# Block 0's first product partly in seven half-size products, and batch 0's local v loaded in 96 rows

## The chip, the cores and the metric

One core of one Trainium2 chip runs the kernel. The metric is the device time of one execution in microseconds (us); the kernel before has a median of 286.13 us over three runs (285.47, 286.13 and 286.18). A core has five engines that run their own instruction streams and wait for each other by semaphores: TensorE (PE, matmuls and transposes; its weight loads are listed as PEld), VectorE (DVE), ScalarE (ACT), GpSimd (POOL) and SyncE (SP). Loads and stores are issued by SP, ACT or POOL and carried out by 16 DMA engines.

## The reference

Attention with two kinds of mask, followed by a two-layer network with the activation h * tanh(softplus(h)) (Mish):

```python
# q, k, v: (8 batches, 8 heads, 576 positions, 64); w_in: 512 x 2048; w_out: 2048 x 512
scores = (q @ k.T) / sqrt(64)
mask_local   = (rel >= 0) & (rel < 32)                     # heads 0..3, rel = row - column
mask_strided = (rel >= 0) & (pos_k % 32 == pos_q % 32)     # heads 4..7
attn = softmax(where(mask, scores, -1e9))
x = concat_heads(attn @ v)            # 4608 tokens x 512
h = x @ w_in
out = (h * tanh(softplus(h))) @ w_out # 4608 x 512, float32
```

## The kernel before

The 4608 tokens are handled as 9 blocks of 512; the attention runs batch by batch (576 tokens), one batch ahead of the blocks, and writes its result transposed into `xT`, a ring of four batches. Everything is in one hand-written order (`manual_schedule`): each engine runs its instructions in the order of the program, and the attention steps of the next batch are put between the matmuls of the second product (`at`, a list of steps by position).

**Local heads.** Heads 0 to 3 work in six windows of 96 queries. A window's keys and values are 128 rows: 32 rows of the window before and its own 96. `vl` holds v in this form, one buffer for even and one for odd batches, with a column of ones after the 64 of each head (it gives the denominators). For batch 0 the windows are fetched whole, overlapping, 128 rows each: heads 0 and 1 in float32 by SP into `vl32` (L876 to L879), which GpSimd casts into `vl` (L906); heads 2 and 3 by GpSimd straight into `vl` (L899 to L903), converted on the way. The 32 rows that would lie before position 0 are set to zero (L888, L907). For the other batches `load_own_v_loc` (L172) fetches only the 96 own rows of each window into rows 32 to 127, and `share_v_loc` (L178) copies rows 96 to 127 of each window to rows 0 to 31 of the next: on GpSimd for batch 1, on ACT from batch 2 on.

**Start.** SP's queue holds two strided heads of k (`st0`) and the local v. GpSimd's queue holds, in this order: the rest of the strided k, strided q, strided v, local k and q, v of heads 2 and 3, `w_in` columns 0:512 and 512:1024, the cast, a memset, `w_in` 1024:1536 and 1536:2048, two memsets, and later the four pieces of `w_out` and the loads of batch 1. PE does some matmuls whose result nobody reads (`unread`, the tile `un`) between batch 0's transposes and scores.

**First product.** In blocks 1 to 8 the first product of most columns is done in the Strassen-Winograd way: with w_in cut in quarters a11, a12, a21, a22 (`w_quarter`: 256 rows of x's features by 768 columns) and xT cut in quarters b11 to b22 (`x_quarter`: 256 features by 256 tokens), seven products of sums (`Sw`, `Sx`, made on DVE by `sums_w_in` and `sums_x`) take the place of eight. In `mlp1` the function `product` (L557) issues one of them as matmuls of 256 columns; results are added up in the accumulators `z[1]`, `z[2]`, `z[3]` and in `z[5]` in SBUF, by ACT copies and DVE adds, and go through Mish on ACT into `gT`. In block 0 all sixteen chunks of 128 hidden columns are done directly instead: `group(g)` (L520) takes chunks 2g and 2g + 1, four matmuls of 512 columns each, and one Mish of 128 x 1024. The strided features (cc 2 and 3) come first for g = 0, 1, 2, as these are ready before the local ones. `sums_w_in()[0:3]` for block 1 is made in this time, over all 768 columns; its last sum, which overwrites a21, comes in block 1.

**Accumulators.** PSUM holds three accumulators of two banks (`acc(0)` to `acc(2)`) and two single banks (`tile_t`). In block 0 `accs = (1, 0, 2)`; group g takes `accs[g % 3]`. Batch 1's attention uses acc 0 and the single banks; the second product of block 0 (`mlp2`) uses acc 2 and acc 1.

**Around the change.** After block 0's first product ACT loads the table for the exponential. The transposes of batch 1's strided k and q (`t_step`, in `T`) follow: T[0] and T[1] at once, T[2] and T[3] after the first four matmuls of `mlp2`, all through the single banks. Then come the scores (`qk`), exponential, mask on DVE, and the products with v (`pv`).

Of the kernel before, what the change touches and what calls it, by code (L numbers as in the profile page):

```python
# [10 lines left out]
F32 = mybir.dt.float32  # L11
BF16 = mybir.dt.bfloat16
# [4 lines left out]
NW = 6  # L17
# [26 lines left out]
def kernel(ctx, tc, q, k, v, moe_w_in, moe_w_out, out):  # L44
# [18 lines left out]
    stm = consts[0:PN, 128 + WQ:128 + WQ + PN]  # L63
    loc_bias = consts[:, 128 + WQ + PN:128 + 2 * WQ + PN]
    stm_bias = consts[0:PN, 128 + 2 * WQ + PN:128 + 2 * WQ + 2 * PN]
    vl32 = const.tile([128, 4, NW, D], F32, name="vl32")
    vsr = const.tile([128, 4, CS * D], BF16, name="vsr")
    ql32 = const.tile([128, 4, CL, D], F32, name="ql32")
    kl32 = const.tile([128, 4, CL, D], F32, name="kl32")
# [36 lines left out]
    def acc(i, name):  # L106

        pool = ps_z[0] if i == 2 else ps_a
        return pool.tile([128, 2, 512], F32, tag=f"acc{i}", name=name)
# [45 lines left out]
    def spread_v_str(b, eng):  # L155
        cast(eng, vs[b % 2][0:PN, :, :, 0:D], vs_raw().rearrange("p h (j d) -> p h j d", d=D))

    def load_v_loc(b):

        w0 = 0
        if b == 0:
            w0 = 1
            nc.sync.dma_start(vl32[32:128, 0, 0, :], v[0, 0, 0:96, :])
        first = v[b, 0:1, 0:1, :].offset + (w0 * WQ - 32) * D
        src = bass.AP(v.tensor, first, [[D, 128], [WQ * D, 4 * NW - w0], [1, D]])
        nc.sync.dma_start(vl32[:].rearrange("p h w d -> p (h w) d")[:, w0:, :], src)  # L170

    def load_own_v_loc(b):  # L172
        for h in range(4):
            nc.gpsimd.dma_start(  # L174
                vl[b % 2][32:128, :, h, 0:D], v[b, h].rearrange("(w p) d -> p w d", p=WQ)
            )
# [17 lines left out]
    def cast(eng, out_, in_):  # L194
        if eng is nc.scalar:
            nc.scalar.copy(out_, in_)  # L196
        else:
            eng.tensor_copy(out_, in_)
# [32 lines left out]
                    by_tile(src[0])[:, hp].rearrange("p i e d -> p (i e d)"),  # L231
                )

    def cast_v_loc(b, eng, i0=0, i1=NW):
        for i in range(i0, i1, 3):
            cast(
                eng, vl[b % 2][:, i:i + 3, :, 0:D],
                vl32[:, :, i:i + 3, :].rearrange("p h w d -> p w h d"),
            )
        if i0 == 0:  # L240
            eng.memset(vl[b % 2][0:32, 0, :, 0:D], 0.0)


    def t_loc(b, which, hp, tr):
        src = by_head((ql if which == "q" else kl)[b % 2])
        for j in range(CL):
# [8 lines left out]
            tr[:, 0:S].rearrange("c (j p) -> c p j", j=CL),  # L255
        )

    def t_step(b, kind, which, hp, eng=None):

        eng = eng or nc.vector  # L260
        tr = tile_t("tr")[:].bitcast(BF16)
        if kind == "s":
            src = (qs if which == "q" else ks)[b % 2]
            for u in range(8):
                h, jj = 2 * hp + u // 4, u % 4
                nc.tensor.transpose(  # L266
                    tr[:, PN * u:PN * u + PN],
                    src[0:PN, h, 128 * jj:128 * jj + 128],
                    ident[0:PN, 0:PN],
                )  # L270
            dst = (qTs if which == "q" else kTs)[:, 8 * SU * hp:8 * SU * hp + 8 * SU]
            cast(
                eng, dst.rearrange("c (u n) -> c u n", u=8)[:, :, 0:PN],
                tr[:, 0:S].rearrange("c (u n) -> c u n", u=8),
            )
        else:
            t_loc(b, which, hp, tr)(eng)

    def unread(n, i_acc=None):

# [168 lines left out]
    def attn_steps(b, x, y):  # L449

        a = Attn(b)
        Q = lambda i_acc, *parts: (lambda: a.qk(parts, i_acc))
        M = lambda kd, i: (lambda: a.mask(kd, i, nc.vector))
        V = lambda kd, i: (lambda: a.pv(kd, i))
        X = lambda kd, hf: (lambda: a.xt(kd, hf))
        s0, s1, sl2, l0, l1 = ("s", 0), ("s", 1), (("s", 2), ("l", 2)), ("l", 0), ("l", 1)
        if x == y:
            T = [(lambda n=n: t_step(b, *T_ORDER[n])) for n in range(4)]

            def t_pair(which):  # L460
                tr = acc(x, "tr")
                copies = [t_loc(b, which, hp, tr[:, hp, :].bitcast(BF16)) for hp in range(2)]
                for copy, eng in zip(copies, (nc.vector, nc.scalar)):
                    copy(eng)

            return [
                T[2:4],
                [Q(x, s0), Q("t", s1), lambda: spread_v_str(b, nc.vector), M(*s0), M(*s1)],
                [],
                [V("s", 0)],  # L470
                [V("s", 1), Q(x, ("s", 2))],
                [V("s", 2), M("s", 2), lambda: t_pair("k")],
                [V("s", 3)],
                [V("s", 4), lambda: t_pair("q")],
                [V("s", 5)],
                [V("s", 6), Q(x, l0)],
                [V("s", 7), M(*l0), Q(x, l1)],
                [X("s", 0), V("l", 0), M(*l1), Q(x, ("l", 2))],
                [X("s", 1), V("l", 1), M("l", 2)],
                [V("l", 2), V("l", 3)],  # L480
                [V("l", 4), V("l", 5)],
                [lambda: a.xt_now(5, nc.vector), lambda: a.xt_later(5)],
            ], T[0:2]
        V2 = lambda kd, i, z: (lambda: a.pv2(kd, i, z))
        G = lambda kd, i: (lambda: a.mask(kd, i, nc.gpsimd))
        l2 = ("l", 2)
        now = -(-(512 * (b + 1) - S * b) // WQ)
        at = [
            [],
            [Q(x, s0), Q(y, s1), Q("t", *sl2), M(*s0), M(*s1), M("s", 2)],  # L490
            [],
            [V2("s", 0, y), G(*l2)],
            [],
            [V2("s", 2, y), Q(x, l0), Q("t", l1), G(*l0), G(*l1)],
            [],
            [V2("s", 4, y), lambda: nc.scalar.preload_act_table(AF.Mish)],
            [],
            [V2("s", 6, y)],
            [V2("l", 0, x)],
            [X("s", 0), V2("l", 2, y), X("s", 1)],  # L500
            [V2("l", 4, x), lambda: a.xt_now(now)],
            [lambda: a.xt_later(now)],
        ]
        return at
# [10 lines left out]
    def mlp1(t, accs):  # L515
# [4 lines left out]
        def group(g, ccs=(2, 3, 0, 1), ps=None, between=None):  # L520
            if g not in held:
                if ps is None:
                    tiles[g] = acc(accs[g % 3 if t == 0 else 0], "psh")
                    ps = [tiles[g][:, u, :] for u in range(2)]
                held[g] = ps
            for u in range(2):
# [13 lines left out]
            if ccs[-1] == 1 and g in tiles:  # L540
                to = gT[:, g::8, :] if t > 0 else gT[:, 2 * g:2 * g + 2, :]
                nc.scalar.activation(to, tiles[g][:], AF.Mish)  # L542
        if t == 0:
            def first_group(g):
                group(g)
                if g == 7:
                    nc.scalar.preload_act_table(AF.Exp)
            halves = [[lambda g=g, c=c: group(g, c) for g in range(3)] for c in ((2, 3), (0, 1))]
            return gT, halves[0], halves[1] + [lambda g=g: first_group(g) for g in range(3, 8)]

        z = {}
        a11, a12, s3, a22 = [w_quarter(i, j) for i in range(2) for j in range(2)]
        s1, s2, s4 = [Sw[:, i] for i in range(3)]
# [27 lines left out]
        def begin():  # L581
# [7 lines left out]
            product(both(z[3]), 0, s1, t1, first=True)  # L589
            sums_x(t, "3")  # L590
            if t == 1:
                sums_w_in()[3]()
            if 1 < t < B - 1:
                spread_v_str(t + 1, nc.vector)
            nc.scalar.copy(z[5][:], z[3][:])
# [1 line left out]
            product([y[1]], 512, a11, b11, first=True)  # L597

        y = {}

        def second():
            for n in range(2):
# [99 lines left out]
    def sums_w_in():  # L702

        a11, a12, a21, a22 = [w_quarter(i, j) for i in range(2) for j in range(2)]
        s1, s2, s4 = [Sw[:, i] for i in range(3)]
        return [
            lambda: sums(s1, a21, a22, ALU.add), lambda: sums(s2, s1, a11, ALU.subtract),
            lambda: sums(s4, a12, s2, ALU.subtract), lambda: sums(a21, a11, a21, ALU.subtract),
        ]

    def x_quarter(t, i, j):
# [157 lines left out]
    with tc.manual_schedule():  # L869
# [3 lines left out]
        st0 = g_pool.tile([128, 16, 512], BF16, tag="gT", name="st0")  # L873
        st0 = st0[0:PN].rearrange("p a b -> p (a b)").bitcast(F32)[:, 0:1024].rearrange("p (h x) -> p h x", h=2)
        nc.sync.dma_start(st0, k[0, 4:6].rearrange("h (p j) d -> p h (j d)", j=CS))
        nc.sync.dma_start(vl32[32:128, 0, 0, :], v[0, 0, 0:96, :])  # L876
        first = v[0, 0:1, 0:1, :].offset + 64 * D
        heads = vl32[:].rearrange("p h w d -> p (h w) d")
        nc.sync.dma_start(heads[:, 1:12, :], bass.AP(v.tensor, first, [[D, 128], [WQ * D, 11], [1, D]]))  # L879
        load_str(0, ks, k, 2)  # L880
        load_str(0, qs, q)
        load_early_v_str(0)
# [2 lines left out]
        Dv.memset(kTs[:, 0:16 * SU].rearrange("c (u n) -> c u n", u=16)[:, :, PN:SU], 0.0)  # L885
        Dv.memset(kTs[:, 16 * SU:], 0.0)
        Dv.memset(kTl[:, :, 0:32], 0.0)
        Dv.memset(vl32[0:32, 0, 0, :], 0.0)  # L888
        for p, n in zip(P_s, (6, 6, 4)):
            Dv.memset(p[:, :, n * PN:], 0.0)  # L890
        for p, n in zip(P_l, (5, 5, 2)):
# [1 line left out]
        for i in range(2):  # L893
            Dv.memset(vs[i][:, :, :, D:D + 1], 1.0)
            Dv.memset(vl[i][:, :, :, D:D + 1], 1.0)
        Dv.memset(vl[0][0:32, 0, :, D:D + 1], 0.0)
        Dv.memset(vl[1][0:32, 0, :, :], 0.0)

        for h in (2, 3):  # L899
            first = v[0, h:h + 1, 0:1, :].offset - 32 * D  # L900
            nc.gpsimd.dma_start(
                vl[0][:, :, h, 0:D], bass.AP(v.tensor, first, [[D, 128], [WQ * D, NW], [1, D]])
            )  # L903
        load_w_in(0, 512)
        load_w_in(512, 1024)
        cast(Po, vl[0][:, :, 0:2, 0:D], vl32[:, 0:2].rearrange("p h w d -> p w h d"))  # L906
        Po.memset(vl[0][0:32, 0, :, 0:D], 0.0)  # L907
        load_w_in(1024, 1536)
        load_w_in(1536, 2048)
        for x in (ks, qs):  # L910
            Po.memset(x[1][64:SU].rearrange("p h x -> p (h x)").bitcast(F32), 0.0)

# [41 lines left out]
        a.xt("s", 1)  # L954
        a.pv2("l", 2, 0)
        a.pv2("l", 4, 2)
        g1s[0]()
        a.xt("l", 0)
        a.xt("l", 1)
        Sc.preload_act_table(AF.Mish)  # L960
        g1s[1]()
        g1s[2]()
        for f in sums_w_in()[0:3]:
            f()
        for x in (ks, qs):
            Po.memset(x[0][64:SU].rearrange("p h x -> p (h x)").bitcast(F32), 0.0)
        load_qk_str(2)
# [92 lines left out]
```

## Time and profile before

The profiled execution took 285.53 us; its span, from the first to the last instruction, is 283.8 us.

| Engine | busy, us | share of the span |
|---|---|---|
| PE | 277.6 | 98% |
| PEld (weight loads) | 217.9 | 77% |
| ACT | 196.4 | 69% |
| DVE | 195.6 | 69% |
| POOL | 109.4 | 39% |

By stage, from the busy time of stretches of the span:

| Stretch, us | what runs | PE | DVE | ACT | POOL | moved, GB/s |
|---|---|---|---|---|---|---|
| 5.00 to 19.80 | batch 0's attention | 13.69 | 6.98 | 8.82 | 8.30 | 193 |
| 19.80 to 34.69 | block 0, first product | 14.75 | 4.33 | 9.85 | 8.43 | 201 |
| 34.69 to 56.25 | block 0, second product, with batch 1's attention | 21.46 | 17.75 | 10.97 | 11.93 | 161 |
| 56.25 to 85.32 | block 1, with batch 2's attention | 29.07 | 25.07 | 24.32 | 12.76 | 169 |

The granted TensorE clock is 1.00 throughout. A line of a timeline reads: start, duration (us), engine, source line, operation, output <- inputs, shape, count, and in brackets the idle time before it with what ended it. Matmuls overlap, so their durations add up to more than the time between their starts; the cost of one in a row of them is the distance of the starts. A line of the chain reads: start, duration, engine, tile, source line, count.

### The profile page before, as it was taken

What the parts mean: (1) busy time and instruction counts of PE and PEld (TensorE: products, weight loads), DVE (VectorE), ACT (ScalarE), POOL (GpSimd) and SP (SyncE); (2) the same over time, 40 slices, a digit from 0 to 9 for tenths busy, and PEclk for the clock granted to TensorE, in tenths of its full rate; (3) what the DMA queues carried; (4) which work ended last, traced back from release to release, by engine and by line L of the source; (5) the groups of instructions that cost most, each with busy time, mean ns of one, the idle gap of its engine ahead of it and who ended that gap; (6) DMA issues with size and microseconds to landing.
All of it is one profiled execution on the core that took longest, in us unless ns stands there. A gap on an engine that the chain in (4) does not pass through costs nothing.

```text
span 283.8 us, 7529 instructions
## 1 busy us (share of the span) xinstructions
PE 277.6 (98%) x3119; PEld 217.9 (77%) x3119; DVE 195.6 (69%) x402; ACT 196.4 (69%) x293; POOL 109.4 (39%) x129
## 2 busy tenths in 40 slices
PE   8899999999999999999999999999999999999994
PEld 3564455686898689868988898789978997888684
DVE  2283078889787777878777778777877767644742
ACT  2578653699857985798679876987798769417820
POOL 8375457308261727253726272535423500000000
PEclk9999999999999999999999999999999999999999
DMA  8999999999998999699989999999969041003004
GB/s 153 187 202 205 197 181 166 132 142 238 170 131 113 217 174 149 136 211 175 152 141 208 153 171 135 222 127 169 148 174 111 3 160 25 0 21 131 0 2 148
DMA packets 103437, 40.28 MB, mean 142 GB/s; under 512 B 85868, under 2 KB 98908, under 8 KB 103404
## 3 DMA queue, kind: packets, MB, share of 16 engines
q1 hardware_dynamic: 65004, 24.40, 50.0%
q0 software_dynamic: 38112, 15.17, 49.3%
q8 instruction: 24, 0.39, 0.7%
q10 hardware_dynamic: 288, 0.25, 0.3%
q14 instruction: 9, 0.07, 0.1%
HBM read 37.01 MB, written 9.44 MB: 164 GB/s over the span
## 4 chain that ended last, share of the span: by engine, by line
PE 92%; DMA 3%; DVE 2%; ACT 1%; issue 0%; POOL 0%; POOLq 0%
PE pso L757 31%; PE psu L562 10%; PE psh L531 10%; PE psv L562 9%; PE psb L562 8%; PE psb L531 5%; PE pso L817 4%; PE po L371 4%; PE pso L790 4%; PE ps L335 4%; DMA qs<-in_q_dram 3%; PE trx L420 1%; DVE x_s L397 1%; PE tr L248 1%; PE trx L435 1%; PE tr L266 1%
## 5 line engine op out<-in xcount | busy, mean ns | idle before, releaser
L757 PEld LDWEIGHTS <-gT 128*128 128x128 bf16 x448 | 41.9, 98 | 5.8
L562 PEld LDWEIGHTS <-w_in 128*128 128x128 bf16 x384 | 37.4, 98 | 8.4
L355 POOL TENSOR_TENSOR Pl<-Pl,consts_sb 128x960 bf16<-128x960 bf16 (+1 forms) x18 | 29.2, 1637 | 35.5 <-issue 22.5
L757 PE MATMUL pso<-w_out,gT 128*128 128x256 bf16 x336 | 41.0, 272 | 0.0
L757 PEld LDWEIGHTS <-Sg 128*128 128x128 bf16 x336 | 31.5, 98 | 4.4
L531 PEld LDWEIGHTS <-w_in 128*128 128x128 bf16 x208 | 20.2, 98 | 16.6 <-issue 0.6
L562 PEld LDWEIGHTS <-Sw 128*128 128x128 bf16 x288 | 28.1, 98 | 3.5 <-DVE Sx L665 0.3
L531 PE MATMUL psh<-xT,w_in 128*128 128x512 bf16 (+1 forms) x136 | 29.4, 366 | 0.2
L196 ACT COPY xT<-trx 128x576 bf16<-128x576 bf16 (+3 forms) x24 | 14.2, 629 | 18.4 <-PE trx L420 12.8
L757 PE MATMUL pso<-Tw,Sg 128*128 128x256 bf16 x224 | 26.7, 273 | 0.0
L196 ACT COPY osb<-pso 128x512 f32<-128x512 f32 (+1 forms) x17 | 9.4, 555 | 20.2 <-PE pso L757 10.8
L174 POOL DMA_DIRECT2D vl<-in_v_dram x28 | 20.6, 742 | 6.2 <-DMA w_out<-in_moe_w_out_dram 2.3
L571 ACT ACTIVATE gT<-psu 128x1024 bf16<-128x1024 f32 x16 | 16.4, 1025 | 8.5 <-PE psu L562 8.5
L397 DVE TENSOR_TENSOR x_s<-po,rden 72x512 bf16<-72x512 f32 x28 | 19.2, 687 | 1.0
L637 POOL COPY mark<-qTl 1x4 bf16<-1x4 bf16 x6 | 2.1, 353 | 45.9 <-DMA qTl<-ql 45.9
L542 ACT ACTIVATE gT<-psh 128x1024 bf16<-128x1024 f32 x16 | 16.2, 1024 | 4.0 <-PE psh L531 3.9
L665 DVE TENSOR_TENSOR Sg<-gT 128x256 bf16<-128x256 bf16 (+2 forms) x32 | 12.8, 422 | 8.0 <-ACT gT L571 6.7
L665 DVE TENSOR_TENSOR psu<-psb,p 128x512 f32<-128x512 f32 x16 | 11.2, 700 | 9.8 <-PE psb L562 9.0
L562 PE MATMUL psu<-xT,w_in 128*128 128x256 bf16 x128 | 17.9, 272 | 0.0
L734 DVE TENSOR_TENSOR p<-pso,p 128x512 f32<-128x512 f32 x14 | 9.6, 686 | 11.8 <-PE pso L757 11.8
L562 PE MATMUL psb<-Sx,w_in 128*128 128x256 bf16 x128 | 17.2, 272 | 0.0
L349 ACT ACTIVATE Ps<-ps 72x864 bf16<-72x864 f32 (+1 forms) x17 | 13.8, 855 | 4.2 <-PE ps L335 4.2
(141 smaller groups left out, 613.7 us busy)
## 6 DMA issues: line engine op xcount, KB each, us to landing
out_dram<-osb SPq DMA_DIRECT2D x9, 512.0 KB, 3.9
out_dram<-p SPq DMA_DIRECT2D x7, 512.0 KB, 3.0
kl<-in_k_dram SPq DMA_DIRECT2D x5, 576.0 KB, 10.2
ql<-in_q_dram SPq DMA_DIRECT2D x5, 576.0 KB, 16.0
qs<-in_q_dram POOLq DMA_DIRECT2D x8, 288.0 KB, 11.1
vsr<-in_v_dram POOLq DMA_DIRECT2D x8, 288.0 KB, 8.6
w_in<-in_moe_w_in_dram POOLq DMA_DIRECT2D x4, 512.0 KB, 9.7
w_out<-in_moe_w_out_dram POOLq DMA_DIRECT2D x4, 512.0 KB, 13.0
```

The lines of the kernel that those rows point to most:

```text
L174: nc.gpsimd.dma_start(vl[b % 2][32:128, :, h, 0:D], v[b, h].rearrange("(w p) d -> p w d", p=WQ))
L196: nc.scalar.copy(out_, in_)
L335: nc.tensor.matmul(by_e[e][:, o:o + w], lhsT=lhsT, rhs=rhs, start=not biased, stop=True, skip_group_check=biased,)
L349: nc.scalar.activation(pt[0:n, :, 0:nw], ps[0:n, :, o0:o0 + nw], AF.Exp, scale=scale)
L355: meng.tensor_tensor(out=pm, in0=pm, in1=mk[0:n, :].unsqueeze(1).unsqueeze(1).to_broadcast([n, 2, nu, w]), op=ALU.mult,)
L397: nc.vector.tensor_tensor(out=dst.rearrange("p e (h d) -> p e h d", h=4), in0=po[0:m, :, :, 0:D], in1=rden[0:m].unsqueeze(3).to_broadcast( ...
L531: nc.tensor.matmul(ps_u[:, o:o + n], lhsT=w_in[:, cc, fc * 128:(fc + 1) * 128], rhs=xT[:, cc, a:a + n], start=(cc == 2 and (o == 0 or len( ...
L542: nc.scalar.activation(to, tiles[g][:], AF.Mish)
L562: nc.tensor.matmul(p[:, 256 * j:256 * j + 256], lhsT=lhs[:, cc, f:f + 128], rhs=rhs[:, cc], start=(first and j == 0 and cc == 0), stop=(la ...
L571: nc.scalar.activation(gT[:, c:c + src.shape[1], 256 * half_t:256 * half_t + 256], src, AF.Mish,)
L665: nc.vector.tensor_tensor(out=out_, in0=in0, in1=in1, op=op)
L757: nc.tensor.matmul(ps[:, pair, :], lhsT=lhs(c, 128 * pair), rhs=rhs(c), start=(first and pair == 0 and c == 0), stop=(last and c == 7), sk ...
```

## The change

Two parts. First, batch 0's local v is fetched like the other batches' (96 rows for each window): SP brings heads 0 and 1 into a smaller `vl32`, whose rows 0 to 31 DVE sets to zero, GpSimd's two loads of heads 2 and 3 become `load_own_v_loc(0, (2, 3))`, and GpSimd copies the shared rows with `share_v_loc(0, Po)` after the cast and the `w_in` loads. The order of the four `w_in` loads becomes 512:1024, 1536:2048, 1024:1536, 0:512, and the last two no longer stand behind the memset L907, which is gone.

Second, block 0's chunks 0 to 3 and 8 to 11 are done by seven products of 512 hidden columns; groups 2, 3, 6 and 7 (chunks 4 to 7 and 12 to 15) stay direct, and come first but for group 7, which is put between the first two products and the others. The sums of w_in are cut in columns 0:512 (made before and in `first_products`, all four) and 512:768 (three in `other_products`, the last in block 1's `begin`). The sums of x for block 0 are new. Batch 1's first two transposes go through acc 0 as a pair (`t_first`) instead of the two single banks.

```diff
-        Dv.memset(vl32[0:32, 0, 0, :], 0.0)
+        Dv.memset(vl32[0:32], 0.0)
...
-        nc.sync.dma_start(vl32[32:128, 0, 0, :], v[0, 0, 0:96, :])
-        first = v[0, 0:1, 0:1, :].offset + 64 * D
-        heads = vl32[:].rearrange("p h w d -> p (h w) d")
-        nc.sync.dma_start(heads[:, 1:12, :], bass.AP(v.tensor, first, [[D, 128], [WQ * D, 11], [1, D]]))
+        nc.sync.dma_start(
+            vl32[32:128].rearrange("p h w d -> p (h w) d"),
+            v[0, 0:2].rearrange("h (w p) d -> p (h w) d", p=WQ),
+        )
...
-        for h in (2, 3):
-            first = v[0, h:h + 1, 0:1, :].offset - 32 * D
-            nc.gpsimd.dma_start(
-                vl[0][:, :, h, 0:D], bass.AP(v.tensor, first, [[D, 128], [WQ * D, NW], [1, D]])
-            )
-        load_w_in(0, 512)
-        load_w_in(512, 1024)
-        cast(Po, vl[0][:, :, 0:2, 0:D], vl32[:, 0:2].rearrange("p h w d -> p w h d"))
-        Po.memset(vl[0][0:32, 0, :, 0:D], 0.0)
-        load_w_in(1024, 1536)
-        load_w_in(1536, 2048)
+        load_own_v_loc(0, (2, 3))
+        load_w_in(512, 1024)
+        load_w_in(1536, 2048)
+        cast(Po, vl[0][:, :, 0:2, 0:D], vl32[:].rearrange("p h w d -> p w h d"))
+        load_w_in(1024, 1536)
+        load_w_in(0, 512)
+        share_v_loc(0, Po)
...
         a.pv2("l", 4, 2)
+        sums_x(0, "1")
         g1s[0]()
...
         g1s[2]()
-        for f in sums_w_in()[0:3]:
-            f()
+        sums_x(0, "234")
+        sums_w_in()[0](slice(0, 512))
...
-                    tiles[g] = acc(accs[g % 3 if t == 0 else 0], "psh")
+                    tiles[g] = acc(accs[{3: 1, 6: 2, 7: 2}.get(g, 0) if t == 0 else 0], "psh")
...
+        def first_products():
+            z[3] = acc(accs[0], "psu")
+            z[2] = [tile_t("psb")[:] for _ in range(2)]
+            z[5] = o_pool.tile([128, 2, DM], F32, tag="osb", name="p5")
+            product(both(z[3]), 0, s1, t1, first=True)
+            for i in (1, 2):
+                sums_w_in()[i](slice(0, 512))
+            nc.vector.tensor_copy(z[5][:], z[3][:])
+            product(z[2], 0, a11, b11, first=True)
+            z[1] = acc(accs[1], "psu")
+            for n in range(2):
+                nc.scalar.copy(z[1][:, n, :], z[2][n])
+            sums_w_in()[3](slice(0, 512))
+
+        def other_products():
+            for n in range(2):
+                product(z[2][n:n + 1], 256 * n, s2, t2)
+                sums(z[3][:, n, :], z[2][n], z[5][:, n, :], ALU.add)
+            product(both(z[1]), 0, a12, b21, last=True)
+            mish(flat(z[1]), 0, 0, 0)
+            product(z[2], 0, s3, t3)
+            for n in range(2):
+                sums(z[5][:, n, :], z[2][n], z[5][:, n, :], ALU.add)
+            product(both(z[3]), 0, s4, b22, last=True)
+            mish(flat(z[3]), 0, 1, 0)
+            for i in range(3):
+                sums_w_in()[i](slice(512, UW))
+            product(z[2], 0, a22, t4, last=True)
+            for n in range(2):
+                mish(z[2][n], 1, 0, 2 * n)
+            mish(flat(z[5]), 1, 1, 0)
+            nc.scalar.preload_act_table(AF.Exp)
+
+        if t == 0:
+            halves = [[lambda g=g, c=c: group(g, c) for g in (2, 3, 6)] for c in ((2, 3), (0, 1))]
+            return gT, halves[0], halves[1] + [first_products, lambda: group(7), other_products]
...
+            def t_first():
+                tr = acc(x, "tr")
+                copies = [t_str(b, w, 0, tr[:, n, :].bitcast(BF16)) for n, w in enumerate("kq")]
+                for copy in copies:
+                    copy(nc.vector)
```

## The prediction

> **What bounds the kernel now.** I read the page's busy line first, then the chain of waits over the whole span, then the timelines of PE, GpSimd (POOL), ACT and DVE for the first 57 us, where all of the change lies.
>
> ```profile
> PE 277.6 (98%) x3119; PEld 217.9 (77%) x3119; DVE 195.6 (69%) x402; ACT 196.4 (69%) x293; POOL 109.4 (39%) x129
> ```
>
> TensorE is busy for 98% of the span. The chain of waits says how that matters for the stages concerned:
>
> ```profile
> 2.22 7.80 DMA qs<-in_q_dram
> 10.07 0.69 PE tr L266 x16
> ...
> 21.74 12.95 PE psh L531 x60
> 34.69 0.52 PE tr L266 x16
> 35.21 0.86 PE pso L790 x4
> ...
> 56.25 1.75 PE psu L562 x16
> ```
>
> (start, duration, what.) The kernel first waits for batch 0's strided q, then does batch 0's attention. Block 0's first product is 64 matmuls of 512 columns; 60 of them take 12.95 us without a gap, so one costs 12.95/60 = 216 ns. Sixteen matmuls of 256 columns take 1.75 us in block 1, so one costs 109 ns. From 34.69 to 56.25 block 0's second product is mixed with batch 1's attention (21.56 us); after that a block takes 29.07 us (56.25 to 85.32) and PE shows no gap in it (29.07 busy of 29.07). So time won before 56 us reaches the end, unless the middle stage takes it back.
>
> The start, on PE:
>
> ```profile
> 8.45 1.24 PE L283 MATMUL un<-Tw 128*128 128x512 bf16 x5
> 10.07 0.69 PE L266 MATMUL tr<-consts_sb,qs 72*128 72x72 bf16 x16 [0.37 <-DMA qs<-in_q_dram]
> ...
> 18.23 0.43 PE L371 MATMUL po<-vl,Pl 128*128 128x65 bf16 x8
> ```
>
> PE stands 0.37 us for q, behind five filler matmuls; the local v is first used at 18.23, with no wait. GpSimd and ACT:
>
> ```profile
> 5.02 2.11 POOL L901 DMA_DIRECT2D vl<-in_v_dram  x2
> 7.11 1.51 POOL L183 DMA_DIRECT2D w_in<-in_moe_w_in_dram  x2
> 8.59 0.88 POOL L198 CAST vl<-vl 128x768 bf16<-128x768 f32 x1
> 15.78 0.30 POOL L907 MEMSET vl<- 32x256 bf16 x1 [6.31 <-DMA vl<-in_v_dram]
> 16.23 1.49 POOL L183 DMA_DIRECT2D w_in<-in_moe_w_in_dram  x2 [0.15 <-issue]
> ...
> 45.38 1.25 POOL L198 COPY vl<-vl 32x1280 bf16<-32x1280 bf16 x1
> ```
>
> ```profile
> 33.00 1.02 ACT L542 ACTIVATE gT<-psh 128x1024 bf16<-128x1024 f32 x1 [0.70 <-PE psh L531]
> 34.73 1.02 ACT L542 ACTIVATE gT<-psh 128x1024 bf16<-128x1024 f32 x1 [0.70 <-PE psh L531]
> 35.77 1.28 ACT L547 ACT_TABLE_LOAD   x1
> 37.87 0.89 ACT L349 ACTIVATE Ps<-ps 72x864 bf16<-72x864 f32 x1 [0.81 <-PE ps L335]
> ```
>
> The reader sees that v of heads 2 and 3 lands at about 15.7, that the second pair of w_in chunks is issued only after it, and that ACT idles 0.81 us before batch 1's first exponential. All times below are in the frame of before until the start is shifted.
>
> **The start: fewer bytes (taken -0.45; between -0.45 and 0).** SP's v load shrinks from 24 + 352 = 376 KB to 2 heads x 576 rows x 256 B = 288 KB; 88 KB go. The 16 DMA engines are full from 4 us on and move about 195 GB/s (windows 4 to 12: 198 and 190). SP's v landed at 1.62 + 6.3 = 7.9, before q's 10.02, so all of the removed bytes stood in front of q: 88 KB / 195 GB/s = 0.45 us. The strided k of heads 2 and 3 (PE waits 0.29 us for it at 7.45) also comes earlier, which moves the fillers up; were they fixed, the gain would end at PE's 0.37. I take 0.45 since all work up to 20.29 on the chain hangs on q or on loads queued behind it (vsr, kl, ql), and these move too. If the engines share otherwise, it is 0. GpSimd's v loads lose another 2 x 24 KB, 0.25 us for what is queued behind them.
>
> **Moved and added on GpSimd's queue (0).** Its order becomes: v of heads 2 and 3, w_in 512:1024 and 1536:2048, the cast, w_in 1024:1536 and 0:512, the copy of 32x1280 shared elements, two memsets, then w_out and batch 1's loads. The memset at 15.78 goes. Each issue costs 0.73 to 0.76. The waits in this queue fit eight loads in flight (w_out at 25.82 waits for the w_in eight places ahead), so the last two w_in wait for q and vsr (10.0, 11.5 before) and not for v. The copy waits for v, 15.0 by the smaller loads, and takes 1.25 as at 45.38: done 16.3. The first user is at 18.23 - 0.45 = 17.8. Cover 1.5 us; behind a late copy stand the two memsets (0.95 each), w_out and batch 1's q, k and v, which were issued from 19.55 and now from about 18.2. DVE's memset grows from 32x64 to 32x768 f32 (0.11 to some 0.8, an estimate from 0.28 for 32x260); DVE idles 2.63 us there for st0.
>
> Chunks now land where before's did, 0.7 earlier. Before's times are issue plus landing, 17.9, 20.5, 22.9 and 25.6 (10.8, 12.6, 6.7 and 8.6 us). So 512: at 17.2, 1536: at 19.8, 1024: at 22.2, 0: at 24.9. The group halves of g = 2 and 3 need the first at 19.3, g = 6 the second at 22.
>
> **The products (-0.82).** Eight chunks x 4 matmuls x 216 ns = 6.91 go; 7 products x 8 matmuls x 109 ns = 6.10 come. This is priced by rows of the same shapes, sums and copies hidden: are they? In before's frame g = 2, 3, 6 end on PE at 25.9, their Mish (1.02 each, from 24.37) at 27.3. Then:
> - s1 x t1 25.9 to 26.8: needs DVE's sums of x (four of 0.34, done 23.6) and Sw's first (chunk 1024:, 22.2). a11 x b11 to 27.6: needs chunk 0: at 26.8 (26.35 with the shift; it lands at 24.9, cover 1.4).
> - DVE copies z5 (two 128x512 f32 rows, 2 x 0.69) by 28.2; ACT copies z1 (2 x 0.57) by 28.5; PE does g = 7 until 29.4.
> - s2 x t2 to 30.2; DVE adds 2 x 0.70 to 31.2 while PE does a12 x b21 (to 31.1); s3 x t3 to 32.0; DVE adds 2 x 0.68 to 33.0 while PE does s4 x b22 (to 32.85); a22 x t4 ends at 33.72. Its second half needs the add of 33.0 and starts at 33.3: the tightest cover, 0.3.
>
> No stall, so PE's end goes from 34.53 to 33.72. If all covers failed by the length of one add, it would cost 0.7.
>
> The Trainium skill (page "TensorE: Matmul & The Clock Gate", section "Back-to-back issue gap") speaks against this: in a stream of weight loads and matmuls it gives about 131 ns for 512 columns, hardly more than one weight load (section "LDWEIGHTS (loading the stationary operand)": 107 ns for 128 columns). By these figures 32 x 131 = 4.2 us go and 56 x 107 = 6.0 come, 1.8 slower (an estimate from that page). The trace's 216 ns contradicts it.
>
> **ACT's tail (+0.2; between 0 and +0.4).** After PE's last matmul (33.72) ACT has Mish of z3 (from 32.9, 1.02), two of 128x512 (0.59 each), z5 (1.06) and the table load (1.28): free at 37.4. PE comes to batch 1's scores after transposes 0.52, matmuls 0.86, transposes 0.52, matmuls 0.86, and the exponential could start at 37.87 - 0.81 = 37.06. It is 0.35 late, mask and first V matmuls behind it had 0.23 to spare (mask 38.79 + 0.60 = 39.39 against 39.63): 0.1 to 0.2 on PE. What follows there hangs on PE again. DVE's three sums of 256 columns lie at 33.0 to 34.0, just ahead of the first transposes' copies at 34.25. Two transposes now share one accumulator, free since z1's Mish (32.2); the other two need the small banks, free at 34.5 and 35.1 against 35.1.
>
> **Sum:** -0.45 - 0.82 + 0.2 = -1.05 us (rounded). The profiled execution took 285.53 (span 283.8 and 1.7 around it); it would become about 284.5, span 282.75. The median shown is 286.13, 0.6 above that execution, so the forecast is 285.1.
>
> **Rivals.**
> - Half of it: q is not earlier (HBM or k sets it) and the tail costs all of 0.4: -0.82 + 0.4 = -0.4, 285.7. For it: the fillers end at 9.5 in any case if k does not move. Against: full DMA engines. 0.20.
> - The best bounds, tail hidden: -1.27, 284.9. 0.05.
> - Slower by the shared rows: v's path to PE at 17.8 gets a new link, DMA, then GpSimd, then PE. DVE works without a break from 14.16 to 17.65. If the copy must wait for that (17.2 shifted) and takes twice its 1.25, it ends at 19.7, and PE stands 1.9: +0.85, 287.0. It decides from an end of 18.85 on, where the gain is gone. Against: the copy at 45.38 took 1.25 beside DVE work. 0.12.
> - The last w_in chunk late: now the last one in line is needed on PE at 26.35; before, PE first read the last one for g = 6, at 25.9 + 3 x 1.73 = 31.1. One more chunk ahead of it (2.6 us) makes it 27.5, PE waits 1.2, and s2 with DVE's copy behind it some more: 286.4 to 287.2. 0.06.
> - Weight loads set the pace (98 ns in the rows): 56 x 98 - 32 x 98 = +2.35 in place of -0.82: 288.2. The rows speak against it. 0.01. The Trainium skill's figures quoted above (page "TensorE: Matmul & The Clock Gate") amount to this.
>
> **Numbers.** The forecast has 0.56, its own range 284.7 to 285.5. What can be told from no change here is 0.3%, 0.86 us: 285.27 to 286.99. Of the forecast 0.45 lies below; with the best case faster has 0.50. Within are 0.11 of it, 0.20 of half, 0.01 of the others: 0.32. Slower 0.18. The range is 284.5 to 286.9.
>
> **What would show it.** q's transposes at 9.6; SP's v at 7.4; the copy on GpSimd ended by 16.5 and no wait at v's first use; the last w_in by 25; 56 matmuls of 256 columns without a gap from 25.5 to 33.3; the exponential some 0.6 earlier; 56.25 becoming 55.2, and blocks of 29.07 as before. A PE wait on GpSimd near 18, on DMA near 26 or on DVE near 32 would make it wrong, and so would a middle stage longer than 22 us.

## The result and the profile after

The changed kernel has a median of 285.01 us (284.90 to 285.73, eight runs) beside 285.89 us (285.43 to 286.40, eight runs) of the kernel before on the same chip. The ratio is 0.9976 with a 95% interval of 0.9968 to 0.9985: 0.69 us less, between 0.43 and 0.91 (the two medians differ by 0.88). The forecast was 285.1. A second set of the same kernel (after_again below) gave 285.16 and a ratio of 0.9980 (0.9971 to 0.9988).

The profiled execution of the changed kernel does not show this gain. It took 285.73, the longest of its eight runs, with a span of 284.0 against 283.8. So the two traces must be compared stage by stage, and not by their ends. The page's first line and the chain of waits of the changed kernel (start, duration, what):

```profile
PE 277.0 (98%) x3128; PEld 220.7 (78%) x3143; DVE 199.1 (70%) x415; ACT 197.3 (69%) x296; POOL 109.6 (39%) x129
```

```profile
1.20 6.58 PE un L258 x16
...
22.27 4.32 PE psh L512 x20
26.59 0.87 PE psu L535 x8
27.46 0.87 PE psb L535 x8
...
34.52 0.52 PE tr L238 x16
```

The chain no longer begins with q's load but with sixteen fillers that take 6.58 us. The first direct groups end at 26.59, the seven products begin there, and batch 1's transposes start at 34.52, against 34.69 before. The first product thus began 0.53 later and ended 0.17 earlier. The start on PE, from its timeline:

```profile
1.20 6.58 PE L258 MATMUL un<-Tw 128*128 128x512 bf16 x16 [1.20 <-DVE Tw L896]
7.62 0.42 PE L238 MATMUL tr<-consts_sb,ks 72*128 72x72 bf16 x8
7.88 0.81 PE L258 MATMUL un<-Tw 128*128 128x512 bf16 x3
8.54 0.42 PE L238 MATMUL tr<-consts_sb,ks 72*128 72x72 bf16 x8
8.79 0.90 PE L281 MATMUL ps<-consts_sb 72*128 72x432 bf16 x4
9.53 1.24 PE L258 MATMUL un<-Tw 128*128 128x512 bf16 x5
10.61 0.68 PE L238 MATMUL tr<-consts_sb,qs 72*128 72x72 bf16 x16
```

PE waits for no load at all: from 1.20 to q's transposes at 10.61 it works through its own string. In before it waited 0.37 for q at 10.07. q landed 7.7 us after its issue at 2.21, at 9.9. GpSimd, with the copy of the shared rows, and ACT's tail:

```profile
10.24 0.75 POOL L169 DMA_DIRECT2D w_in<-in_moe_w_in_dram  x1 [0.75 <-DMA qs<-in_q_dram]
11.83 0.86 POOL L169 DMA_DIRECT2D w_in<-in_moe_w_in_dram  x1 [0.85 <-DMA vsr<-in_v_dram]
15.54 1.25 POOL L184 COPY vl<-vl 32x1280 bf16<-32x1280 bf16 x1 [2.85 <-DMA vl<-in_v_dram]
```

```profile
33.69 1.02 ACT L544 ACTIVATE gT<-psu 128x1024 bf16<-128x1024 f32 x1 [0.76 <-PE psu L535]
34.61 1.08 ACT L544 ACTIVATE gT<-psb 128x512 bf16<-128x512 f32 x2
35.56 1.07 ACT L544 ACTIVATE gT<-p 128x1024 bf16<-128x1024 f32 x1
36.65 1.28 ACT L605 ACT_TABLE_LOAD   x1
37.94 0.89 ACT L324 ACTIVATE Ps<-ps 72x864 bf16<-72x864 f32 x1
```

The last two w_in wait for q and for vsr, as forecast from eight loads in flight; the copy ends at 16.8, two us ahead of v's first use at 18.76. ACT has no idle time left before the exponential (0.81 before).

The table gives the stages of every profile taken. The first column is the landing of batch 0's strided q. The next four go by the starts of PE's matmuls: q's first transpose; the first product (first matmul of `psh` to the transposes of batch 1's k); the middle (from there to block 1's first `psu`); blocks 3 and 4 together. The end runs from the landing of the last output to the end of the span. From q's transposes to the first `psh` all but three of them take 9.69 to 9.73 us (products_only 9.86, v_pool 11.17, v_pool_pad 10.73); blocks 1 and 2 take 29.06 to 29.07 each.

| Run | q lands | q starts | first product | middle | blocks 3, 4 | end | span |
|---|---|---|---|---|---|---|---|
| before | 10.02 | 10.07 | 14.76 | 21.56 | 57.92 | 1.40 | 283.8 |
| after | 9.95 | 10.61 | 14.06 | 21.57 | 58.20 | 1.62 | 284.0 |
| after_again | 9.90 | 9.95 | 14.06 | 21.58 | 58.20 | 1.60 | 283.3 |
| v_only | 9.85 | 9.89 | 14.76 | 21.56 | 57.92 | 1.60 | 283.6 |
| products_only | 10.43 | 10.48 | 14.01 | 21.60 | 58.20 | 1.41 | 283.8 |
| fill11 | 9.53 | 10.13 | 14.05 | 21.57 | 58.20 | 1.62 | 283.5 |
| fill_less | 10.01 | 10.06 | 14.06 | 21.58 | 58.20 | 1.61 | 283.5 |
| shift3 | 9.33 | 9.38 | 14.06 | 21.58 | 57.92 | 1.60 | 282.5 |
| tail_plus | 9.94 | 9.98 | 14.05 | 22.66 | 57.92 | 1.62 | 284.2 |
| no_sp_v | 8.04 | 9.53 | 14.06 | 21.57 | 58.20 | 1.55 | 282.8 |
| v_pool_16 | 7.92 | 10.49 | 14.06 | 21.57 | 58.20 | 1.68 | 283.9 |
| v_pool | 7.42 | 7.97 | 14.23 | 21.85 | 58.20 | 1.66 | 283.3 |
| v_pool_pad | 7.96 | 8.21 | 14.06 | 22.02 | 57.92 | 1.67 | 282.8 |
| before_pad2 | 10.15 | 10.36 | 14.76 | 21.57 | 58.20 | 1.40 | 284.2 |

Four things stand out. The stages repeat to a few hundredths. The change takes 0.70 from the first product and adds 0.28 in blocks 3 and 4. It adds 0.2 at the very end (0.15 to 0.28 in every kernel with v's part). And q's start differs from execution to execution by more than any of these.

### The profile page after: what moved, and what is told of

The parts are those of the page before. It is cut to its first block, busy times and chain, and to the rows that moved or that the text cites. A ratio compares the mean times of both kernels' runs of the same rounds, so it can differ in the third digit from the quotient of the medians.

```text
span 284.0 us, 7580 instructions
## 1 busy us (share of the span) xinstructions
PE 277.0 (98%) x3128; PEld 220.7 (78%) x3143; DVE 199.1 (70%) x415; ACT 197.3 (69%) x296; POOL 109.6 (39%) x129
## 4 chain that ended last, share of the span: by engine, by line
PE 86%; DMA 7%; DVE 2%; ACT 2%; SPq 1%; issue 1%; POOL 0%; DVEq 0%; POOLq 0%
PE pso L769 26%; PE psu L535 10%; PE psb L535 9%; PE psv L535 8%; PE psh L512 7%; DMA ql<-in_q_dram 6%; PE pso L829 4%; PE psb L512 4%; PE pso L802 4%; PE po L346 4%; PE un L258 3%; PE ps L310 3%; DMA kTl<-kl 1%; PE trx L395 1%; PE tr L238 1%; ACT Pl L324 1%
## 5 line engine op out<-in xcount | busy, mean ns | idle before, releaser
L535 PEld LDWEIGHTS <-Sw 128*128 128x128 bf16 x312 | 30.5, 98 | 4.0
L544 ACT ACTIVATE gT<-psu 128x1024 bf16<-128x1024 f32 x18 | 18.5, 1025 | 9.9 <-PE psu L535 9.9
L160 POOL DMA_DIRECT2D vl<-in_v_dram x30 | 22.6, 760 | 6.9 <-DMA w_out<-in_moe_w_out_dram 2.6
L512 PE MATMUL psh<-xT,w_in 128*128 128x512 bf16 (+1 forms) x95 | 22.2, 361 | 0.6
L675 DVE TENSOR_TENSOR psu<-psb,p 128x512 f32<-128x512 f32 x18 | 12.6, 700 | 14.5 <-PE psb L535 13.5
L535 PE MATMUL psb<-Sx,w_in 128*128 128x256 bf16 x144 | 19.4, 272 | 0.0
L535 PE MATMUL psu<-xT,w_in 128*128 128x256 bf16 x136 | 18.9, 272 | 0.2 <-ACT psb L560 0.2
L512 PE MATMUL psb<-xT,w_in 128*128 128x512 bf16 (+1 forms) x72 | 16.4, 355 | 0.0
L802 PE MATMUL pso<-w_out,gT 128*128 128x512 bf16 x59 | 15.8, 380 | 0.4 <-issue 0.2
## 6 DMA issues: line engine op xcount, KB each, us to landing
ql<-in_q_dram SPq DMA_DIRECT2D x5, 576.0 KB, 16.3
```

What stands on the lines that cost most here:

```text
L160: nc.gpsimd.dma_start(vl[b % 2][32:128, :, h, 0:D], v[b, h].rearrange("(w p) d -> p w d", p=WQ))
L512: nc.tensor.matmul(ps_u[:, o:o + n], lhsT=w_in[:, cc, fc * 128:(fc + 1) * 128], rhs=xT[:, cc, a:a + n], start=(cc == 2 and (o == 0 or len( ...
L535: nc.tensor.matmul(p[:, 256 * j:256 * j + 256], lhsT=lhs[:, cc, f:f + 128], rhs=rhs[:, cc], start=(first and j == 0 and cc == 0), stop=(la ...
L544: nc.scalar.activation(gT[:, c:c + src.shape[1], 256 * half_t:256 * half_t + 256], src, AF.Mish,)
L675: nc.vector.tensor_tensor(out=out_, in0=in0, in1=in1, op=op)
L802: nc.tensor.matmul(p[:, ot % 2, :], lhsT=gT[:, fc, 128 * ot:128 * ot + 128], rhs=w_out[:, fc, :], start=(fc == 0), stop=(fc == 15),)
```

## The experiments

Four kernels ran together on one chip first (medians, and ratios to the kernel before of that set).

**v_only**: the first part of the change alone, on the kernel before.

```diff
-        for h in (2, 3):
...
-        Po.memset(vl[0][0:32, 0, :, 0:D], 0.0)
+        load_own_v_loc(0, (2, 3))
+        load_w_in(0, 512)
...
+        share_v_loc(0, Po)
```

> Only the first part of the change: batch 0's v in 96 rows and the shared rows copied by GpSimd; the first product and the order of the w_in loads as before. Theory A (bytes, as in the prediction): q lands 0.45 us earlier and everything after it moves, so the time falls by 0.4 to 0.5 us. Theory B (what the trace of the changed kernel suggests: q landed at 2.21 + 7.7 = 9.9 against 10.0, while SP's v landed 1.25 us earlier): q does not follow the bytes, so the time stays within 0.15 us of before; q's landing is again 7.7 to 7.8 us after its issue.

285.59 against 285.83, ratio 0.9999 (0.9990 to 1.0007). Theory B's time came out: v's part alone is worth nothing that shows (-0.03, between -0.29 and +0.20). q landed at 9.85, and k 6.3 us after its issue at 1.34, at 7.6 (7.4 in before). But the total does not show that q ignores the bytes: in this profile q starts 0.18 earlier than in before's, and the end is 0.20 longer.

**products_only**: the second part alone, with the new order of the w_in loads.

```diff
-        load_own_v_loc(0, (2, 3))
+        for h in (2, 3):
...
         load_w_in(512, 1024)
         load_w_in(1536, 2048)
...
-        share_v_loc(0, Po)
+        Po.memset(vl[0][0:32, 0, :, 0:D], 0.0)
```

> Only the second part: the seven products, with v loaded as before (128 rows, memset L907) and the new order of the w_in loads, the last two of which stay behind the memset. Sum of the prediction: -0.82 for the products and +0.2 for ACT's tail, -0.6. By the two traces' own stages (first product 14.76 before, 14.06 after; the stage behind it 21.13 and 21.14): -0.7. If v's part carries most of the gain (theory A), this is -0.4 or less. The last chunk of w_in lands near 25.6; if that is too late for the second product, PE shows a wait near 27 and the gain is gone.

285.32, ratio 0.9984 (0.9975 to 0.9992): -0.46, between -0.71 and -0.23. Its stages from the first `psh` on, against before's, give -0.75 + 0.04 + 0.28 = -0.43; its end is before's. No wait of PE shows near 27, so the last chunk of w_in was in time even behind the memset.

**after_again**: the changed kernel, unchanged.

> The changed kernel once more, for a second profile. Theory W: in the first profile the sixteen filler matmuls at the start took 427 ns each until 7.6 us (in before's 216 ns from 4.0 us on), which is a matter of the single execution and not of the change: in this profile, or in another of this set, they speed up at another time, q's transposes start between 9.6 and 10.1, and the span is 283.0 to 283.4. Rival: the slow fillers come with the change (DVE's longer memset or other work at the start); then they take 6.6 us again and q's transposes start at 10.6. The stall of 0.28 us in block 4 (a chain through the transposes by DMA) is likewise gone by theory W and there again by its rival.

285.16, ratio 0.9980 (0.9971 to 0.9988). The fillers took 5.41 here and q started at 9.95: the slow fillers were a matter of the execution. The second half of theory W fell: block 4's 0.28 was there again, and in every kernel with the products except the three in which the number of ACT instructions had been changed.

**fill11**: 11 fillers in place of 16.

```diff
-        unread(16)
+        unread(11)
```

> The changed kernel with 11 fillers in place of 16 at the start. At 427 ns they end by 1.2 + 4.7 = 5.9, when the first strided k is ready (5.87), even if they never speed up. Theory W1: the fillers only stand in the way in executions in which they stay slow; the slow executions vanish, the fast ones stay: median 0 to 0.2 us below the changed kernel, and q's transposes start at its landing, 9.9 to 10.0. Rival: with less work in the first 6 us the matmuls speed up later still, the work from 6 to 12 us runs slow, and the time rises by 0.3 to 1 us.

285.11, ratio 0.9976 (0.9967 to 0.9986), not to be told from the changed kernel. In its profile the loads were late (k 6.7 us after its issue), so PE waited for k, and q's start was again k's transposes plus 2.1, at 10.13, though q had landed at 9.53.

The second set turned to the pause, the start and the tail.

**shift3**: three tiny ACT copies while ACT is idle.

```diff
+        for _ in range(3):
+            Sc.copy(pad[:], consts[0:1, 0:4])
```

> The changed kernel with three tiny ACT copies (1 x 4) added near 8 us, where ACT is idle. In every run with the products so far the ACT copy from the first product's accumulator in block 4 (the first of the two, ACT's instruction 191) starts 0.62 us after ACT's last work instead of 0.34, and block 4 is 0.28 longer (58.2 us for blocks 3 and 4 together against 57.9 in before and with v's part alone); a load of instructions follows right behind it. Theory P: a pause at a fixed place in ACT's instruction stream, moved onto a critical copy by the three ACT instructions that the change adds. Then three more move it off: 57.9 for the two blocks, and a median 0.2 to 0.3 below the changed kernel. Rival: block 4 is longer because of the rotated output buffers or the data loads; then it stays 58.2.

284.99, ratio 0.9972 (0.9959 to 0.9985); blocks 3 and 4 are back at 57.92. ACT's copy in block 4, from the timelines of the changed kernel and of shift3 (the bracket gives the idle time before it):

```profile
144.44 1.06 ACT L560 COPY psb<-psu 128x512 f32<-128x512 f32 x2 [0.62 <-PE psu L535]
```

```profile
142.96 1.06 ACT L561 COPY psb<-psu 128x512 f32<-128x512 f32 x2 [0.34 <-PE psu L536]
```

0.62 against 0.34: the 0.28 is idle time of ACT right before a copy that the next product waits for. The median's gain (0.02 and 0.17 against the two sets of the changed kernel) is less than the 0.28 and within the spread of the runs; the stage shows the 0.28 without doubt.

**before_pad2**, run last: the kernel before with two such copies.

> The kernel before with two tiny ACT copies (1 x 4) added at the start, nothing of the change. Theory P: they move the copy of block 4 from the 189th to the 191st entry of ACT's stream, so blocks 3 and 4 take 58.20 in place of 57.92 and the median rises by 0.28. Rival (the pause belongs to the products): 57.92 and no difference.

286.20 against 285.76, ratio 1.0012 (1.0003 to 1.0021), blocks 3 and 4 at 58.20:

```profile
144.89 1.06 ACT L588 COPY psb<-psu 128x512 f32<-128x512 f32 x2 [0.62 <-PE psu L563]
```

Two copies in ACT's idle time at 8 us cost the kernel before 0.28 us at 144 us. The pause belongs to a place in ACT's stream, the 191st entry of the trace (counted from 0, waits included), and not to the products. A second pause of this kind stood at the 319th entry of tail_plus and v_pool_pad, 128 further, where it cost nothing.

**fill_less**: 11 and 2 fillers in place of 16 and 5.

```diff
-        unread(16)
+        unread(11)
...
-        unread(5, 2)
+        unread(2, 2)
```

> The changed kernel with 11 in place of 16 fillers at the start and 2 in place of 5 between the strided k and q. With 5, q's transposes come 2.2 to 2.3 us after the second half of k, whether q is there or not. Theory K: k's landing (7.4 to 8.0) and the fillers behind it set q's start, and this is why fewer bytes of v did not help; with 2 fillers the start is q's landing (9.5 to 9.9), 0.2 to 0.5 earlier than in the first two profiles of the changed kernel, median 0.1 to 0.4 lower. Rival: what follows hangs on other loads (strided v, local k, at 11.5 and 12.7), so that the gain ends there, and the time stays within 0.1; or the matmuls fall back to 427 ns for 512 columns, and it rises.

285.13, ratio 0.9974 (0.9965 to 0.9984), the changed kernel's. In the profile PE was through with its string by 9.2 and then q itself was late (2.2 + 7.8 = 10.0). So q's landing set the start, as theory K had it, but the landing was no earlier and the forecast gain did not come: fewer fillers alone only uncover the load.

**tail_plus**: z5's Mish twice.

```diff
             mish(flat(z[5]), 1, 1, 0)
+            mish(flat(z[5]), 1, 1, 0)
             nc.scalar.preload_act_table(AF.Exp)
```

> The changed kernel with z5's Mish done twice (one more ACT instruction of 1.06 us in the tail behind the first product). The prediction charged the tail with 0.2; the stage behind the first product took 21.14 against 21.13, so it cost nothing that shows. Theory T (the tail is on PE's path, its cover is used up: the first mask ends at 39.46, its user starts at 39.52): 0.8 to 1.1 us longer. Rival (the stage has slack of its own further on and takes the delay back): below 0.4.

286.01, ratio 1.0010 (1.0000 to 1.0019). The middle takes 22.66 in place of 21.57: 1.09 more for an instruction of about 1.06; the pause of 0.28 in block 4 is gone in this kernel. Theory T: the cover of ACT's tail is used up to the last tenth, though the change itself pays nothing for it.

**no_sp_v**: SP's load of v left out, so that this kernel leaves heads 0 and 1 of batch 0's local v at zero.

> The changed kernel without SP's load of v: heads 0 and 1 of batch 0's local v are zero, so these 288 KB are not moved. By bytes (theory A) 288 KB at 195 GB/s is 1.5 us: strided k lands at 6.1 and q at 8.4. Theory K: k's landing hardly follows the bytes (7.4 in before, 7.5 to 8.0 with 88 KB less) but its own issue and its place behind st0; k lands at 7.0 to 7.6, q between 8.4 and 9.5, and PE starts q's transposes 2.2 to 2.3 us after k.

A single execution: 284.60. k landed at 1.33 + 4.1 = 5.4 and q at 2.21 + 5.8 = 8.0, about 2 us earlier for 288 KB, more than theory A's 1.5; theory K, with k at 7.0 to 7.6, fell. But PE came to q at 9.53, one and a half us after it had landed: sixteen fillers until 6.55, then k's transposes, fillers, bias and fillers.

The last set put the two together.

**v_pool_16** and **v_pool**: all four heads of batch 0's v by GpSimd behind local q, without and with fewer fillers.

```diff
-        nc.sync.dma_start(
-            vl32[32:128].rearrange("p h w d -> p (h w) d"),
...
-        load_own_v_loc(0, (2, 3))
+        load_own_v_loc(0)
```

> The changed kernel with all four heads of batch 0's local v loaded by GpSimd behind local q (no load by SP, no cast), fillers as they are. Without SP's v in front, k landed at 5.4 and q at 8.0 (the run without SP's load), but PE began q's transposes at 9.53 all the same. Theory F (two floors, the string of fillers and q's landing, the later one counts): k near 5.4, q near 8.0, PE at q between 9.4 and 10.5 by the fillers alone, median within 0.4 below the changed kernel. Rival (loads alone set it): PE at q by 8.6 and 1.0 to 1.5 less time.

> The same with 11 and 2 fillers in place of 16 and 5. Fewer fillers alone gained nothing (fill_less: q's transposes at 10.06, at its landing), an early q alone nothing by theory F; together both floors fall: q's transposes at 8.0 to 8.8, the rest of the start 9.70 as in all runs, and the time 1.0 to 1.6 below the changed kernel (283.4 to 284.1). Rival 1: with less work ahead, matmuls of 512 columns stay at 427 ns longer and take it back, gain below 0.5. Rival 2: the v that now lands last, or the last chunk of w_in, ends the wait of PE (seen near 17 or 26), gain below 0.8.

v_pool_16: 285.24, ratio 0.9977 (0.9964 to 0.9989). k and q landed at 5.6 and 7.9; PE came to q at 10.49. v_pool: 285.01, ratio 0.9975 (0.9966 to 0.9984), with q at 7.97. PE's timelines, v_pool_16 first:

```profile
10.49 0.69 PE L237 MATMUL tr<-consts_sb,qs 72*128 72x72 bf16 x16
```

```profile
7.97 0.68 PE L237 MATMUL tr<-consts_sb,qs 72*128 72x72 bf16 x16
...
11.53 0.70 PE L223 MATMUL tr<-consts_sb,kl 96*64 96x96 bf16 x24 [0.73 <-DMA kl<-in_k_dram]
...
18.55 0.23 PE L394 MATMUL trx<-consts_sb,x_s 72*128 72x72 bf16 x2 [0.74 <-issue]
```

Theory F held for the start: only with both floors lowered does q move, by 2.0 against after_again. The time did not follow (rival 2, in another place than named): local k is the next to be late (0.73), 0.74 goes in a stop of PE that the profile puts down to nothing, so that the way to the first product takes 11.17 in place of 9.70; the first product takes 0.17 and the middle 0.28 more. The forecast 283.4 to 284.1 was missed.

**v_pool_pad**: the same with one tiny ACT copy.

```diff
+            Sc.copy(pad[:], consts[0:1, 0:4])
```

> The same with one tiny ACT copy more at the start. Theory P (a pause of 0.28 wherever a fixed place in ACT's stream, the 191st entry of the trace, is a copy that PE waits for): one entry more moves it off, as the extra Mish did (blocks 3 and 4 together 57.92), and the time is 0.28 below the kernel without it, 283.1 to 283.9. Rival: no difference.

284.70 (283.76 to 285.26), ratio 0.9959 (0.9943 to 0.9975), the lowest median of the kernels that do the whole computation, but above the forecast 283.1 to 283.9. Blocks 3 and 4 are at 57.92; the middle takes 0.45 more than in the changed kernel, for which no cause is shown. It beats the kernel before by 0.7 to 1.6 us; its lead over the changed kernel, 0.3 by the medians of different sets, is inside the intervals.

## Why the prediction was right

The time and the direction came out, the sum only in part. Of its three terms the products were sized a little too large, the tail far too large, and the start is not shown at its size; two costs were missing, 0.28 in block 4 and 0.20 at the end.

**What bounds the kernel.** Right. Blocks 1 and 2 take 29.06 to 29.07 in every profile, so what is won before 56 us reaches the end, less the pause in block 4 and the longer end.

**"The start: fewer bytes (taken -0.45)": not shown at this size, and v's part has a cost that the sum left out.** v's part as a change of its own measured -0.03 (-0.29 to +0.20), so as the worth of that part -0.45 failed. A part of the difference is the end. PE's last matmuls, in before and in the changed kernel:

```profile
278.25 1.91 PE L817 MATMUL pso<-Tw,gT 128*128 128x256 bf16 x16
```

```profile
278.25 1.91 PE L829 MATMUL pso<-Tw,gT 128*128 128x256 bf16 x16
```

They lie at the same time, but the spans are 283.8 and 284.0. The end takes 1.40 to 1.41 in the three kernels that load v in 128 rows and 1.60 to 1.62 in the seven with v's part and SP's load; no run tried why. Without these 0.20, v_only's start would be worth about -0.23, between -0.49 and 0 (an estimate from its measured time), so -0.45 is neither shown nor excluded.

The landings speak for the sum's picture more than against it. q lands at 10.02, 10.15 and 10.43 in the three profiles with 376 KB in SP's queue and at 9.33 to 10.01 in the seven with 288 KB, 0.41 earlier on average. The profiles of before and of the changed kernel, taken alone, show only 0.07 of this. By queue, in before (packets, MB, share of 16 engines; q1 holds SP's loads, q0 GpSimd's), from 4 to 5 us and from 7 to 8 us:

```profile
q1 hardware_dynamic: 848, 0.21, 119.6%
q0 software_dynamic: 51, 0.00, 4.0%
```

```profile
q0 software_dynamic: 193, 0.19, 129.7%
```

From 4 to 5 us SP's loads fill the engines and GpSimd's move next to nothing; from 7 to 8 us GpSimd's alone move 0.19 MB. So SP's bytes do stand in front of GpSimd's in this profile. The rate of 195 GB/s is no constant, though: in v_pool, where GpSimd's loads have the engines to themselves from 4 us on, it is 141 and 151 GB/s in the two stretches from 4 to 6 us.

What the sum did not count is that q's landing is only one of two floors. PE's string of fillers holds q's transposes until 10.61 in the changed kernel's first profile (q had landed at 9.95), and until 9.53 and 10.49 in no_sp_v and v_pool_16 (8.04 and 7.92). The prediction named this floor as a bound and as a rival ("the fillers end at 9.5 in any case") and chose the other value.

**The products (-0.82).** The mechanism was right, the size -0.70. Most of the missing 0.12 sits at DVE's adds, 0.09 of it, one product ahead of the cover that the prediction called tightest. From the timelines of PE and DVE of the changed kernel:

```profile
31.65 1.13 PE L535 MATMUL psb<-Sx,w_in 128*128 128x256 bf16 x8
32.61 1.04 PE L535 MATMUL psu<-xT,Sw 128*128 128x256 bf16 x8
```

```profile
30.59 1.53 DVE L675 TENSOR_TENSOR psu<-psb,p 128x512 f32<-128x512 f32 x2 [1.27 <-PE psb L535]
```

The other groups of eight start 0.87 apart, this one is followed after 0.96. Its second half overwrites what DVE's second add reads, and the two adds end at 30.59 + 1.53 = 32.12. The sum had charged 1.4 for them from the end of the first four matmuls; they begin 0.25 after it (29.90 + 0.44 = 30.34). The Trainium skill's 131 ns for a matmul of 512 columns (page "TensorE: Matmul & The Clock Gate", section "Back-to-back issue gap") stays refuted here: twenty take 4.32 us, 216 ns each, and the chain shows 0.87 for eight of 256 columns, 109 ns each.

**ACT's tail (+0.2).** 0.01. The exponential came 37.94 - 34.36 = 3.58 after batch 1's first transposes against 37.87 - 34.53 = 3.34, so it was 0.24 late (0.35 in the forecast). The first matmul with V started 5.16 and 5.10 after them, and those 0.06 were made good later in the stage. That there is no more to give was shown by tail_plus.

**GpSimd's queue, w_in, the shared rows (0).** Right: copy 15.54 to 16.8 (forecast 15.0 to 16.3), DVE's wait for the last chunk until 25.03 (forecast 24.9), no wait of PE on either.

**Missing: +0.28** by the pause on ACT. **And +0.20** at the end by v's part. From the first `psh` on the second part is worth -0.70 + 0.01 + 0.28 = -0.41, which products_only repeats (-0.46 measured); with the end the whole change is worth -0.21 there. (Before's profile also has 0.13 more in block 5, 29.02 against 28.89 to 28.90 in the thirteen others; this is taken for a matter of its one execution.) The changed kernel measured -0.69 and -0.57, which leaves 0.4 to 0.5 for the start; v_only leaves 0.2. With intervals of a quarter us to either side they do not contradict each other, and none settles the term. So the forecast's -1.05 was too large chiefly by the two missing costs, while the tail's 0.2 that did not come hid part of them; the sign was carried by the products. That 285.01 lies 0.1 from the forecast is in part luck: the forecast set out from 286.13, the median of three runs, and the eight runs beside the changed kernel have 285.89.

## What to carry to other kernels

A load that comes earlier helps only if nothing else stands in front of its user: here PE's own warm-up string ended at the same time as the load, and neither alone could be shortened with profit. A profile is one draw: where the start differs by a us between executions, compare stages, not ends, take a second profile before a difference is put down to the change, and let the steps behind the last matmul be one of the stages. And when a few instructions are added to an engine, look for a new short stop far away, at a wait that had no slack; a harmless instruction more may remove it.

## What the hardware showed unasked

**The matmuls' speed at the start.** The listed clock is 1.00 in these stretches, but the first fillers take 427 ns for 512 columns and then, from one to the next, 216. The switch came between 3.73 (shift3) and 7.15 us (the changed kernel's first profile), that is 2.5 to 6.0 us after the first matmul, in the twelve profiles in which it falls among the fillers (in fill11 and v_pool_pad all eleven are slow); sixteen fillers take 4.93 to 6.58 us. The Trainium skill (page "TensorE: Matmul & The Clock Gate", section "Part 1: The HAM clock gate (the "warmup" mystery)") describes a gate that opens after a busy window of 3.4 us that runs freely, and gives about 4 us with 500 ns to either side. The traces fit the gate (a step by half) and the window's length (the spread is 3.4 us), not the 500 ns; the listed clock does not show the gate.

**A pause in ACT's stream.** 0.28 us where the 191st entry of the trace is a copy that was waited for, in each of nine profiles of that kind, and in none of the other five. In the changed kernel's second profile a load of instructions of 0.31 us begins at 143.96, right behind that copy's start at 143.83. But in the other eight it comes between 0.13 us before the copy's start and 1.2 us after, and kernels without the pause have one too. So it is not shown as the cause, which stays open.

**A stop of PE.** In v_pool PE stands 0.74 us between two transposes of one group (line above); v_pool_pad has none there. Its cause stays open.
